# Moving one GpSimd copy, one PSUM copy and one group of transposes where batch 2 begins

## The chip, the cores and the metric

The kernel runs on one core of a Trainium2 chip. A core has five engines that run side by side, each working through its own queue in order: PE (TensorE, the matmuls and transposes), DVE (VectorE), ACT (ScalarE), POOL (GpSimd) and SP (SyncE, here only a queue that issues DMAs). They wait for each other through semaphores. PE writes to PSUM, which has eight banks; the other engines read it there. The metric is the device time of one execution in microseconds, as the median of several runs.

## The reference

For each of 8 batches and 8 heads there is x (512 rows of 64) and a state (32 rows of 64). Attention runs in both directions, and its result is the input of a two-layer network with GELU:

```python
a = softmax(x @ state.T / 8);      xread = a @ state     # 512 rows
a2 = softmax(state @ x.T / 8);     sread = a2 @ x        # 32 rows
y = concatenate([xread, sread])                          # heads side by side: 4352 rows of 512
out = gelu(y @ w_in) @ w_out                             # w_in 512x2048, w_out 2048x512
```

The output has 8 x 544 = 4352 rows of 512 in float32.

## The kernel before

The kernel never forms xread. Per batch it multiplies the state by w_in first (`p_mm`, L421: the result P has 256 rows, one for each head and state row, and 2048 columns) and then the attention weights by P. So the steps of one batch are these.

- `load_x` brings x of the batch into the tile xb by a GpSimd-issued DMA that also converts it to bf16. `rearr` (L224, two GpSimd copies) brings it into the order that the transposing DMA wants, the tile x4. `xtr_dma` (L277, issued on SP) transposes x4 into xT.
- `state_prep` (L159 and L165) transposes the state on PE, five batches at once for batches 3 to 7, and VectorE copies the result into sbd. The state comes by its own load, st_bf.
- `scores` (L330) multiplies xT by sbd and takes the exponential on ScalarE. `norm` (L350 to L353) sums, takes the reciprocal and scales on VectorE, once for each half of the heads; the scaling is L353. `atr_dma` (L373, on SP) transposes the weights a into AT.
- P is copied out of PSUM to bf16, by ScalarE for one half of the rows and VectorE for the other.
- `M(k)` is one block of the first layer (L484, two 128x512 matmuls and a GELU on ScalarE, L491). Blocks 16 to 31 belong to batch 1, block 32 is the first of batch 2.
- `U` (L510) and `X` (L581) are pieces of the second layer. Batch 0 goes plainly; from batch 1 on the second layer is done with seven products of quarter matrices (`X(b, "3")` and so on) whose operands VectorE sums first (`g_sum`, L575, and `w_sums`, L547).
- `rearr_ones` (L234, GpSimd) copies x into a third layout, xo, for `sread` (L384), which comes a whole batch later.
- `hold_for(b, m)` (L902) is a 128x1 GpSimd copy out of the output of one GELU. Its only purpose is the order: what follows it on GpSimd doesn't start before that GELU.

The order of the work is written out by hand: the kernel is a list of these calls, and each engine takes its instructions in the order of the list. The banks are part of that order. Four banks of PSUM rotate among the tiles of `ftile` (the blocks' hp, the scores, the state transposes, some P tiles); each new tile takes the bank that comes free first in the order of the list and waits until its former reader has finished. Four further banks have fixed names, o0 to o3.

Around the change, P of batch 2 is made in four tiles: p0[0] in bank o1, p0[1] in o3, p1[0] in o2, and p1[1] in a rotating bank. Three are copied by VectorE (L1093), p0[0] by ScalarE (L1095). In the kernel before, the state transposes for batches 3 to 7 take the rotating bank that p1[1] leaves, block 30 takes that of block 27, and block 31 that of block 28. `X(1, "6")` takes bank o3.

On SP's queue, `atr_dma(2)` stands ahead of `xtr_dma(3)`. On GpSimd's queue, the order before is: the load of batch 3's x, the load of the last five states, the two copies of batch 3's x (which wait for the load), `hold_for(1, 12)`, the two copies of batch 2's x into xo, `hold_for(2, 0)`, and the load of batch 4's x.

Of the kernel before, what the change touches and what calls it, by code (L numbers as in the profile page):

```python
# [17 lines left out]
def kernel(  # L18
# [8 lines left out]
    nc = tc.nc  # L27
# [51 lines left out]
    hold = persist.tile([128, 1], BF16, name="hold")  # L79
# [75 lines left out]
    def state_prep(b0, b1, pool=ps_f, tag="f"):  # L155
        n = b1 - b0
        ps = pool.tile([128, n, HC, NS], BF16, name="st_ps", tag=tag)
        for b in range(b0, b1):
            nc.tensor.transpose(  # L159
                ps[:, b - b0, :, :].rearrange("p c n -> p (c n)"),  # L160
                st_bf[:, b, :, :].rearrange("q t d -> q (t d)"),
                ident,
            )
        for t in range(2):
            nc.vector.tensor_copy(  # L165
                out=sbd[64 * t:64 * t + 64, b0:b1, :, 32 * t:32 * t + 32].rearrange(
                    "d b c n -> d (b c) n"
                ),
                in_=ps[64 * t:64 * t + 64, :, :, :].rearrange("d b c n -> d (b c) n"),
            )  # L170
# [32 lines left out]
    atts = {}  # L203

    def begin(b):
        A = Att()
        atts[b] = A
        A.x4 = x4s[b % 2]
        A.xo = xos[b % 2]
        if b > 0:  # L210
            A.xT = att.tile([128, SJ, HC, 128], BF16, name="xT", tag="xT")
# [8 lines left out]
    def rearr(b):  # L220
        A = atts[b]
        src = xbs[b].rearrange("p (t c) (j d) -> p t c j d", t=2, d=D)
        for t in range(2):
            nc.gpsimd.tensor_copy(  # L224
                out=A.x4[:, :, :, 64 * t:64 * t + 64].rearrange("p j c d -> p c j d"),
                in_=src[:, t],
            )

    def rearr_ones(b):
        A = atts[b]  # L230
        eng = nc.vector if b < 2 else nc.gpsimd
        src = xbs[b].rearrange("p (t c) (j d) -> p t c j d", t=2, d=D)
        for t in range(2):
            eng.tensor_copy(  # L234
                out=A.xo[:, :, :, 2 + 64 * t:66 + 64 * t].rearrange("p j c d -> p c j d"),
                in_=src[:, t],
            )
# [37 lines left out]
    def xtr_dma(b):  # L275
        A = atts[b]
        nc.sync.dma_start_transpose(  # L277
            out=A.xT.rearrange("p j c n -> p (j c) n"),
            in_=A.x4.rearrange("p j c n -> p (j c n)"),
        )  # L280
# [63 lines left out]
    def norm(b, half):  # L344
        A = atts[b]
        G = SJ * 2
        hs = slice(64 * half, 64 * half + 64)
        e4 = A.e[:, :, hs].rearrange("p g (c n) -> p g c n", n=NS)
        cs = att.tile([128, G, 2], FP32, name="cs", tag="cs")
        nc.vector.reduce_sum(out=cs, in_=e4, axis=AX.X)  # L350
        ics = att.tile([128, G, 2], FP32, name="ics", tag="ics")
        nc.vector.reciprocal(out=ics, in_=cs)
        nc.vector.tensor_tensor(  # L353
            out=A.a[:, :, hs].rearrange("p g (c n) -> p g c n", n=NS),
            in0=e4,
            in1=ics[:, :, :].to_broadcast((128, G, 2, NS)),
            op=ALU.mult,
        )
# [11 lines left out]
    def atr_dma(b):  # L370
        A = atts[b]
        A.AT = att.tile([128, SJ, 2, 128], BF16, name="AT", tag="AT")
        nc.sync.dma_start_transpose(  # L373
            out=A.AT.rearrange("p j t n -> p (j t) n"), in_=A.a
        )
# [39 lines left out]
    def p_mm(b, f, tiles):  # L415
        if b not in Ps:
            Ps[b] = att.tile([128, 2, d_ff], BF16, name="P", tag="P")
        ps = [tiles([128, 512], "p_ps") for t in range(2)]
        for c in range(HC):
            for t in range(2):  # L420
                nc.tensor.matmul(  # L421
                    ps[t][32 * c:32 * c + 32, :],
                    lhsT=sbd[64 * t:64 * t + 64, b, c, 32 * t:32 * t + 32],
                    rhs=w_in_bf[64 * t:64 * t + 64, c, f * 512:(f + 1) * 512],
                    start=True,
                    stop=True,
                )
        return ps
# [50 lines left out]
    def mm1(b, m):  # L479
        if m == 0:  # L480
            gs[b] = gpool.tile([128, MC, S], BF16, name="g", tag="g")
        hp = ps_f.tile([128, S], FP32, name="hp", tag="f")
        for t in range(2):
            nc.tensor.matmul(  # L484
                hp,
                lhsT=Ps[b][:, t, m * 128:(m + 1) * 128],
                rhs=atts[b].AT[:, :, t, :],
                start=(t == 0),
                stop=(t == 1),
            )  # L490
        nc.scalar.activation(out=gs[b][:, m, :], in_=hp, func=AF.Gelu)  # L491
# [57 lines left out]
    def w_sums(i):  # L549
        (b11, b12), (b21, b22) = w_q  # L550
        w_add(*(
            ("3", b12, b22, ALU.subtract),
            ("4", b21, b11, ALU.subtract),
            ("6", b11, b12, ALU.add),
            ("1", b11, b22, ALU.add),
            ("7", b21, b22, ALU.add),
        )[i])
# [343 lines left out]
    def hold_for(b, m):  # L901
        nc.gpsimd.tensor_copy(out=hold, in_=gs[b][:, m, 0:1])  # L902


    def M(*ms):
        for m in ms:
            mm1(m // MC, m % MC)
# [156 lines left out]
    U(13)  # L1064
    state_prep(2, 3, ps_o, "o3")
    w_sums(1)
    begin(3)
    rearr(3)
    M(18, 19)
    M(20, 21)  # L1070
    U(14)
# [6 lines left out]
    norm(2, 0)  # L1078
    norm(2, 1)
    atr_dma(2)  # L1080
    xtr_dma(3)
    M(24, 25)
    M(26, 27)
# [5 lines left out]

    p0 = p_mm(2, 0, home)  # L1090
    p1 = p_mm(2, 1, home)
    for f, t, ps in ((0, 1, p0), (1, 1, p1), (1, 0, p1)):
        nc.vector.tensor_copy(out=Ps[2][:, t, f * 512:(f + 1) * 512], in_=ps[t])  # L1093
    M(28, 29)
    nc.scalar.copy(out=Ps[2][:, 0, 0:512], in_=p0[0])  # L1095
    hold_for(1, 12)
    rearr_ones(2)
    state_prep(3, B)
    M(30, 31)
    nc.scalar.copy(out=xs[1, "s3"], in_=xs[1, 0])  # L1100
    X(1, "6")
    w_sums(3)
# [124 lines left out]
```

## Time and profile before

| what | value |
| --- | --- |
| median of five runs | 205.52 us (204.42 to 206.72) |
| profiled execution | 206.02 us, of which the span from the first to the last instruction is 204.3 us |
| mean granted TensorE clock | 0.999 |
| busy: PE, DVE, ACT, POOL | 196.7 (96%), 156.8 (77%), 135.5 (66%), 70.5 (35%) us |
| chain that ended last | PE 86%, DMA 5%, POOL 4%, DVE 2%, ACT 1% |
| load of batch 3's x | issued at 37.13 us, landed 10.6 us later |
| load of the last five states | issued at 38.01 us, landed 11.4 us later |

All times in the profile are in microseconds from the start of the span unless marked ns. A busy PE isn't necessarily a PE at its peak, since matmuls overlap and their ends are modelled. An instruction's idle time names what released it last. "To landing" is the time from a DMA's issue until its completion was signalled. The chain that ended last is followed backwards from the last instruction, at each step to what released it; only time on this chain can be won.

### The profile page before, as it was taken

The numbers are of one execution on the slowest core, as the hardware profiler recorded it, in microseconds if no ns is written. First come the engines' busy times: TensorE is split into PE (matmuls) and PEld (weight loads), VectorE is DVE, ScalarE is ACT, GpSimd is POOL, SyncE is SP. The second block draws the span as 40 slices with busy tenths as digits, with TensorE's granted clock in tenths as the row PEclk, the third lists the DMA queues.
The fourth block names the chain that finished last, engine by engine and source line by source line (L and its number), as shares of the span: only waits on it lengthen the run. The fifth ranks groups of instructions, "written<-read, shape, count | busy, mean of one in ns | idle before, by whom it ended". The sixth has DMA issues, their size and how long they took to land.

```text
span 204.3 us, 4903 instructions
## 1 busy us (share of the span) xinstructions
PE 196.7 (96%) x2033; PEld 133.4 (65%) x2039; DVE 156.8 (77%) x254; ACT 135.5 (66%) x240; POOL 70.5 (35%) x76
## 2 busy tenths in 40 slices
PE   7897999998999999999999999999999999999994
PEld 2442644463776667766875777667776787878893
DVE  2943677879699888977897787778778988895882
ACT  3783776689796679675966787587847666864120
POOL 8973403406619545371625702340220002200000
PEclk9999999999999999999999999999999999999999
DMA  6999997796586697836584404660107001040135
GB/s 197 187 148 203 205 200 124 120 218 162 106 119 131 188 129 85 177 138 70 58 164 126 120 0 108 77 181 3 51 3 205 3 0 55 0 157 0 51 104 157
DMA packets 40566, 23.16 MB, mean 113 GB/s; under 512 B 21856, under 2 KB 39136, under 8 KB 40544
## 3 DMA queue, kind: packets, MB, share of 16 engines
q0 software_dynamic: 13984, 8.10, 30.0%
q1 hardware_dynamic: 25872, 14.36, 28.1%
q10 hardware_dynamic: 688, 0.39, 0.6%
q8 instruction: 16, 0.26, 0.5%
q14 instruction: 6, 0.05, 0.1%
HBM read 17.30 MB, written 8.91 MB: 128 GB/s over the span
## 4 chain that ended last, share of the span: by engine, by line
PE 86%; DMA 5%; POOL 4%; DVE 2%; ACT 1%; issue 0%; POOLq 0%
PE xp L581 40%; PE hp L484 25%; DMA w_in_bf<-in_moe_w_in_dram 5%; PE p_ps L421 4%; PE op L526 4%; PE sp L788 3%; PE rp L854 3%; PE xp L693 2%; POOL w_in_bf L105 2%; PE pt L330 1%; PE sr L384 1%; PE op L510 1%; POOL sbd L95 1%; POOL w_out_bf L113 1%; DVE a L353 1%; DVE cs L350 1%
## 5 line engine op out<-in xcount | busy, mean ns | idle before, releaser
L491 ACT ACTIVATE g<-hp 128x512 bf16<-128x512 f32 x124 | 67.0, 603 | 27.1 <-PE hp L484 20.4
L484 PE MATMUL hp<-AT,P 128*128 128x512 bf16 x248 | 63.0, 379 | 0.1
L581 PEld LDWEIGHTS <-gsum 128*128 128x128 bf16 x528 | 51.1, 98 | 12.4 <-issue 1.9
L575 DVE TENSOR_TENSOR gsum<-g 128x2048 bf16<-128x2048 bf16 x35 | 45.9, 1326 | 0.9 <-ACT g L491 0.9
L581 PE MATMUL xp<-ws,gsum 128*128 128x256 bf16 x304 | 36.3, 273 | 0.0
L484 PEld LDWEIGHTS <-P 128*128 128x128 bf16 x248 | 22.9, 98 | 20.0 <-issue 2.6
L581 PE MATMUL xp<-ws,g 128*128 128x256 bf16 x224 | 26.7, 273 | 0.0
L581 PE MATMUL xp<-w_out_bf,gsum 128*128 128x256 bf16 x224 | 26.6, 273 | 0.0
L581 PEld LDWEIGHTS <-g 128*128 128x128 bf16 x224 | 21.8, 98 | 4.9 <-issue 0.2
L433 DVE CAST P<-p_ps 128x512 bf16<-128x512 f32 x29 | 18.8, 684 | 5.7 <-PE p_ps L421 5.6
L636 POOL TENSOR_TENSOR u<-s,oh 128x512 f32<-128x512 f32 x6 | 8.9, 1490 | 40.4 <-ACT oh L633 40.4
L224 POOL COPY x<-xb 128x1024 bf16<-128x1024 bf16 x12 | 13.1, 1121 | 23.2 <-DMA xb<-in_x_dram 23.2
L432 ACT CAST P<-p_ps 128x512 bf16<-128x512 f32 x29 | 15.9, 598 | 7.4 <-PE p_ps L421 7.1
L234 POOL COPY xo<-xb 128x1024 bf16<-128x1024 bf16 x12 | 15.9, 1354 | 4.2 <-PE sr L384 4.2
L600 POOL TENSOR_TENSOR v<-q,oh 128x512 f32<-128x512 f32 x6 | 8.7, 1447 | 20.8 <-ACT oh L638 20.8
L421 PE MATMUL p_ps<-w_in_bf,sbd 64*32 64x512 bf16 x248 | 10.8, 383 | 1.3 <-DMA w_in_bf<-in_moe_w_in_dram 1.3
L526 PE MATMUL op<-w_out_bf,g 128*128 128x512 bf16 x44 | 11.1, 380 | 0.5 <-issue 0.3
L353 DVE TENSOR_TENSOR a<-e,ics 128x512 bf16<-128x512 bf16 x14 | 10.4, 743 | 0.5
L350 DVE TENSOR_REDUCE cs<-e 128x16 f32<-128x512 bf16 x14 | 9.5, 677 | 0.6 <-ACT e L337 0.5
L411 DVE COPY XSR<-srT 128x128 bf16<-128x128 bf16 x8 | 5.7, 759 | 5.1 <-PE srT L408 5.1
L337 ACT ACT_TABLE_LOAD x7 | 9.0, 1283 | 0.1
L491 ACT ACT_TABLE_LOAD x7 | 9.0, 1283 | 0.1
(128 smaller groups left out, 225.9 us busy)
## 6 DMA issues: line engine op xcount, KB each, us to landing
out_dram<-oh SPq DMA_DIRECT2D x15, 256.0 KB, 2.8
xb<-in_x_dram POOLq DMA_DIRECT2D x7, 512.0 KB, 6.0
out_dram<-oh SPq DMA_DIRECT2D x6, 512.0 KB, 3.0
w_in_bf<-in_moe_w_in_dram POOLq DMA_DIRECT2D x6, 256.0 KB, 11.7
out_dram<-osb SPq DMA_DIRECT2D x5, 256.0 KB, 6.1
w_out_bf<-in_moe_w_out_dram POOLq DMA_DIRECT2D x4, 256.0 KB, 9.0
w_out_bf<-in_moe_w_out_dram POOLq DMA_DIRECT2D x2, 512.0 KB, 12.7
x0f<-in_x_dram SPq DMA_DIRECT2D x3, 256.0 KB, 3.8
```

What stands on the lines that cost most here:

```text
L224: nc.gpsimd.tensor_copy(out=A.x4[:, :, :, 64 * t:64 * t + 64].rearrange("p j c d -> p c j d"), in_=src[:, t],)
L234: eng.tensor_copy(out=A.xo[:, :, :, 2 + 64 * t:66 + 64 * t].rearrange("p j c d -> p c j d"), in_=src[:, t],)
L350: nc.vector.reduce_sum(out=cs, in_=e4, axis=AX.X)
L353: nc.vector.tensor_tensor(out=A.a[:, :, hs].rearrange("p g (c n) -> p g c n", n=NS), in0=e4, in1=ics[:, :, :].to_broadcast((128, G, 2, NS) ...
L421: nc.tensor.matmul(ps[t][32 * c:32 * c + 32, :], lhsT=sbd[64 * t:64 * t + 64, b, c, 32 * t:32 * t + 32], rhs=w_in_bf[64 * t:64 * t + 64, c ...
L432: nc.scalar.copy(out=dst[:, 0, :], in_=ps[0])
L433: nc.vector.tensor_copy(out=dst[:, 1, :], in_=ps[1])
L484: nc.tensor.matmul(hp, lhsT=Ps[b][:, t, m * 128:(m + 1) * 128], rhs=atts[b].AT[:, :, t, :], start=(t == 0), stop=(t == 1),)
L491: nc.scalar.activation(out=gs[b][:, m, :], in_=hp, func=AF.Gelu)
L526: nc.tensor.matmul(ops[b, j], lhsT=gs[b][:, m, j * 128:(j + 1) * 128], rhs=w_out_bf[:, m, :], start=(m == 0), stop=(m == MC - 1),)
L575: nc.vector.tensor_tensor(out=t, in0=g_q(b, h0, k0), in1=g_q(b, h1, k1), op=op)
L581: nc.tensor.matmul(ps[:, j - js[0], :], lhsT=lhs[:, m, 128 * j:128 * j + 128], rhs=rhs[:, m, :], start=(first and j == js[0] and m == 0), ...
```

## The change

There are three edits, all in the written-out list; no arithmetic is changed.

1. `begin(3)` and `rearr(3)` move from behind `w_sums(1)` to behind `atr_dma(2)`, and a 128x1 GpSimd copy out of batch 2's weights a is put ahead of them. That copy reads one column of the half that the second `norm` scales, so the two GpSimd copies of batch 3's x now wait for that scaling.
2. Of the three VectorE copies of P, that of p1[1] becomes the first; p0[1] is second, p1[0] third as before.
3. Blocks 30 and 31 move ahead of the state transposes. By the rotation of the banks block 30 now takes the bank that p1[1] leaves, block 31 that of block 27, and the transposes that of block 28.

```diff
     state_prep(2, 3, ps_o, "o3")
     w_sums(1)
-    begin(3)
-    rearr(3)
     M(18, 19)
     M(20, 21)
...
     norm(2, 0)
     norm(2, 1)
     atr_dma(2)
+    nc.gpsimd.tensor_copy(out=hold, in_=atts[2].a[:, 0, 64:65])
+    begin(3)
+    rearr(3)
     xtr_dma(3)
     M(24, 25)
     M(26, 27)
...
     p0 = p_mm(2, 0, home)
     p1 = p_mm(2, 1, home)
-    for f, t, ps in ((0, 1, p0), (1, 1, p1), (1, 0, p1)):
+    for f, t, ps in ((1, 1, p1), (0, 1, p0), (1, 0, p1)):
         nc.vector.tensor_copy(out=Ps[2][:, t, f * 512:(f + 1) * 512], in_=ps[t])
     M(28, 29)
     nc.scalar.copy(out=Ps[2][:, 0, 0:512], in_=p0[0])
     hold_for(1, 12)
     rearr_ones(2)
+    M(30, 31)
     state_prep(3, B)
-    M(30, 31)
     nc.scalar.copy(out=xs[1, "s3"], in_=xs[1, 0])
     X(1, "6")
     w_sums(3)
```

## The prediction

> **What bounds the kernel now.** I read the chain that ended last first, because it says which engine's time is the program's time. 86% of it is PE, and from 49.67 us to the end it is PE without a break: the idle groups name no PE wait after the one at 49.67, and TensorE's granted clock is 0.999. So a change here is worth only what it does to the time at which PE gets through the stretch from 47 to 56 us; whatever it saves or loses there shifts everything behind it by the same amount. The chain in order of time over that stretch (start, length, piece):
>
> ```profile
> 47.73 0.69 DVE a L353
> 48.42 1.21 DVE P L1093 x2
> 49.63 0.04 issue
> 49.67 0.44 PE st_ps L159 x5
> 50.11 0.86 PE hp L484 x4
> 50.98 1.75 PE xp L581 x16
> ...
> 55.78 0.47 PE pt L330 x16
> ```
>
> The chain leaves PE only here: two of the three P copies on VectorE (L1093) hold the state transposes (L159). Next I read the timelines of the engines over the same stretch (start, length, engine, line; in brackets the idle time before it and what ended it):
>
> ```profile
> 48.02 1.08 PE L484 MATMUL hp<-AT,P 128*128 128x512 bf16 x4
> 49.67 0.44 PE L159 MATMUL st_ps<-ident,st_bf 128*128 128x128 bf16 x5 [0.58 <-DVE P L1093]
> ...
> 48.94 1.28 DVE L1093 CAST P<-p_ps 128x512 bf16<-128x512 f32 x2
> 49.54 0.68 DVE L1093 CAST P<-p_ps 128x512 bf16<-128x512 f32 x1
> ...
> 47.83 2.48 POOL L224 COPY x<-xb 128x1024 bf16<-128x1024 bf16 x2 [8.87 <-DMA xb<-in_x_dram]
> 50.37 3.03 POOL L234 COPY xo<-xb 128x1024 bf16<-128x1024 bf16 x2
> ...
> 48.49 1.25 SPq L373 DMA_TRANSPOSE AT<-a  x1
> 50.34 1.85 SPq L277 DMA_TRANSPOSE xT<-x  x1
> ```
>
> To be seen: blocks 28 and 29 end, PE sits 0.58 us, then the transposes run. GpSimd's copy of batch 3's x starts at 47.83, the moment its load lands, and its end (47.83 + 2.48 = 50.31) releases the transposing DMA at 50.34. Last, the groups by tile: for xT of batch 3, and for the two-input sums on VectorE beside a GpSimd copy elsewhere in the run:
>
> ```profile
> L277 SPq DMA_TRANSPOSE xT<-x x1: 1848/1848/1848, 50.3 to 50.3; - x1
> DMA to landing us min/median/max: 4.6/4.6/4.6
> ...
> 77.94 2.03 POOL L224 COPY x<-xb 128x1024 bf16<-128x1024 bf16 x2
> 78.21 2.84 DVE L575 TENSOR_TENSOR gsum<-g 128x2048 bf16<-128x2048 bf16 x1
> ```
>
> xT lands at 50.34 + 4.6 = 54.94. The first weight load from it (scores of batch 3, L330) is at 55.50, so this transfer has only 0.56 us of slack. That number decides the case.
>
> **Copy order and the blocks put ahead of the transposes.** Nothing is added on PE or VectorE; the same instructions stand in another order. The last matmul of block 29 starts at 48.72; matmuls of this shape follow each other every 0.215 us (four in 0.86), so PE could go on at 48.94. Before, the transposes took the bank of p1[1], whose copy is second: it starts at 48.94 and PE went on at 49.67, that is 0.73 us after the start of the copy. After, block 30 takes that bank and the copy is first: it starts at 48.34, so block 30 starts at 48.34 + 0.73 = 49.07. Block 31 needs the GELU of block 27 (starts at 48.33, 0.60 long: 48.93), which is there. The two blocks take 0.86 us, to 49.93. The transposes now take block 28's bank; its GELU starts at 48.81 and ends at 49.41, so no wait, and the load of st_bf, for whose landing the weight load of the transposes waited until 49.47, is in too. Five transposes take 0.28 us (49.67 to 49.95, where block 30 followed). X(1, "6") then starts at 49.93 + 0.28 = 50.21, against 49.95 + 0.86 = 50.81: **0.60 us gained**. What the new order makes late is covered: the copy of p0[1], now second, ends at 49.62, ahead of X(1, "6") (50.21), which takes its bank; the copies into sbd end some 0.25 us later (51.4), 1.5 us ahead of their next reader on PE (52.92). If the copy order alone were made, the landing of st_bf would be next at 49.47, and only 0.2 us would be gained; the moved blocks cover it.
>
> **What is late next.** Block 32 would start at 52.56 - 0.60 = 51.96; its AT was issued at 48.49 and landed 3.1 us later, at 51.59: 0.37 us to spare. The other five AT transfers took 3.5 to 5.3 us, so this margin is thin, but those ran beside other queues' traffic. The scores of batch 3 come at 55.50 - 0.60 = 54.90, and xT already lands at 54.94 before: the slack is gone even if nothing is done to it.
>
> **The copy of batch 3's x, held.** One GpSimd instruction is added: hold, 128x1, of the rows 0.19 to 0.37 us long, which waits for the second scaling (L353, 47.73 + 0.69 = 48.42). Behind it on GpSimd stand both x copies, then hold_for(1, 12), both xo copies and the next x load; on SP's queue xtr_dma(3) waits for the x copies. An earlier hold ran 0.14 us behind its GELU, and its successor started 0.13 us behind it (50.24, 50.37). So the copies start at 48.42 + 0.1 + 0.13 = 48.65 (48.8 with the longest hold), 0.8 us later. But the first copy took 1.495 us against 1.037 for the shortest of this line, because it ran into the scaling until 48.42; held, it doesn't. Both together then take 2.03 us, as at 77.94: the end is 50.68 to 50.85, I take 50.73. xtr_dma(3) goes at 50.76 instead of 50.34, **0.42 us later**. Its duration is not shown for that start: the six transfers of L277 landed 4.2, 4.4, 4.6, 4.9, 5.4 and 6.1 us after issue. Bounds are 4.2 and 6.1; I take 4.6, the row of the same batch, as nothing else moves on the DMA engines at that time (their share is 0 from 54.25 on, and AT's packets are through at 51.05). xT lands at 55.36, and PE waits 55.36 - 54.90 = **0.46 us lost**. The xo copies slip to 50.9 and beside the weight sum of VectorE at 51.4; at worst (both copies first, as at 78.21) that sum ends near 54.2, the P copy behind it at 54.8 and the operand sum at 56.0, still ahead of X(1, "5") at 56.35. The next x load goes near 54.8 rather than 54.49; xT of batch 4 landed over 9 us before its use. So these cost nothing.
>
> One rule speaks to the hold. The rows come first: at 78.21 a two-input sum of 1.21 us (the shortest of its line) took 2.84, having come 0.27 us behind two GpSimd copies that together last 2.03; it was held 1.63 us. At 47.83 the copy came 0.10 us behind the scaling, and the copy was held. The Trainium skill, "SBUF — State Buffer", section "Who interferes with whom", says that a VectorE instruction with two SBUF inputs and a GpSimd instruction that reads SBUF exclude each other, and that whichever starts first keeps the port for its whole instruction. By that rule the sum at 78.21 would have been free after the first copy, an estimated 0.8 us, and an x copy ahead of the scaling would cost the kernel before one copy at most. The row at 78.21 shows both copies. In the profiled execution the scaling came first, so this price is not in the sum; where the load lands 0.1 us or more sooner, the row puts it at 0 to 1.63 us on the path through AT and the P copies.
>
> **Sum.** -0.60 + 0.46 = -0.14 us. The profiled execution took 206.02 us (span 204.3 and 1.7 around it), so it would become 205.88. It is 0.50 above the median of the five runs, which lie from 204.42 to 206.72; against the median the forecast is 205.52 - 0.14 = **205.4 us**, its own range 205.2 (xT in 4.4 us) to 205.5 (the longest hold, or xT in 4.7).
>
> **Rivals.**
> (a) The whole gain or more. If xT lands 4.2 us after issue (54.96), PE waits 0.06 and 0.54 us are gained: 205.0. If the load of batch 3's x commonly lands sooner than in the profiled execution, the kernel before also pays for the copy ahead of the scaling: between 0 and 1.63 us by the row at 78.21, and with the middle, 0.8, that gives 204.2. For it: the margin seen was 0.10 us. Against: only one execution shows the landing.
> (b) Slower: the held copy makes xT the bound. PE reaches the scores later than before as soon as 50.76 + d is over 55.50, that is d over 4.74 us. Three of the six transfers are over that. With d = 5.4, the scores come at 56.16: 0.66 us lost, 206.2; if the kernel before had the same d, the difference is 0.42, 205.9. Against: the slow ones had output traffic near them.
> (c) The change does not do what it says: the copy order still leaves PE waiting, since GELUs 24 to 28 sit end to end on ScalarE (46.88 to 49.41). Then it gains 0 to 0.1 and loses nothing beyond the slack of 0.56: 205.5.
>
> **Chances.** Forecast 0.40, (a) 0.28, (b) 0.27, (c) 0.05. About 1% of the time (2.06 us) is what a measurement of this kernel can tell from no change; no case reaches that alone. Only landings that shift several waits at once would, so faster 0.05, same 0.90, slower 0.05. The range runs from (a) with most of the port's middle price (205.0 - 0.6; 204.42 is also the fastest run before) to (b) with 0.66 and 0.2 for the scatter of a median over few runs that lie 2.3 us apart: 204.4 to 206.4.
>
> **What the profile after would show.** Right: no PE idle time ahead of L159; block 30 near 49.07; X(1, "6") near 50.2; L224's two copies 2.0 to 2.1 us long from about 48.65; a new PE wait of about 0.5 us at L330 near 54.9, released by xT's transfer. Wrong: PE waiting at block 32 for AT (a late transpose); no wait at L330 (case a); a wait over 1.06 us there (case b); L224 still at 1.5 us, or GpSimd's hold much later than 48.6.

## The result and the profile after

The changed kernel takes 206.12 us (median of 43 runs) against 205.74 us for the kernel before (80 runs). The ratio is 1.0018 with a 95% interval of 1.0003 to 1.0032: **slower by 0.4 us, between 0.06 and 0.66**. The forecast was a gain of 0.14 us. So the time lies inside the range, on the wrong side, and the case that came true is rival (b). That (b)'s 206.2 us lies near the measured time is partly luck: it stood for a loss of 0.66 us from 205.52, and the kernel before came out at 205.74.

The profiled execution took 207.21 us, with a span of 205.4 us. Its chain that ended last, in order of time (start, length, piece), no longer leaves PE for the P copies. It leaves it for the copy of batch 3's x and the transfer of xT:

```profile
47.48 0.70 DVE a L353
...
48.30 0.19 POOL hold L1079
48.49 0.74 POOL x L224
49.23 0.18 issue
49.41 1.04 POOL x L224
50.45 0.03 POOL hold L902
50.47 5.77 DMA xT<-x
56.24 0.05 issue
56.29 0.64 PE pt L330 x16
```

The timelines of PE, VectorE, GpSimd and SP over the same stretch:

```profile
47.76 2.08 PE L484 MATMUL hp<-AT,P 128*128 128x512 bf16 x8
49.68 0.44 PE L159 MATMUL st_ps<-ident,st_bf 128*128 128x128 bf16 x5
49.96 1.91 PE L581 MATMUL xp<-ws,gsum 128*128 128x256 bf16 x16
...
56.29 0.64 PE L330 MATMUL pt<-sbd,xT 128*128 128x64 bf16 x16 [1.36 <-DMA xT<-x]
...
48.42 2.03 POOL L224 COPY x<-xb 128x1024 bf16<-128x1024 bf16 x2
...
50.47 1.93 SPq L277 DMA_TRANSPOSE xT<-x  x1
```

PE runs blocks 28 to 31, the transposes and X(1, "6") without a gap: the stall of 0.58 us is gone. In its place PE waits 1.36 us at the scores of batch 3. The group by tile says why:

```profile
L277 SPq DMA_TRANSPOSE xT<-x x1: 1927/1927/1927, 50.5 to 50.5; - x1
DMA to landing us min/median/max: 5.8/5.8/5.8
```

The transfer took 5.8 us, not 4.6. The profiled executions in this document differ by up to 2.4 us in how soon batch 2 gets there, ahead of the stretch that the change is about. Below I therefore use one measure that leaves the start out: the **stretch** from batch 2's first sum on VectorE (L350) to the scores of batch 3 on PE (L330). Before it is 55.62 - 45.11 = 10.51 us, after 56.29 - 44.86 = 11.43 us.

### The profile page after: what moved, and what is told of

It reads as the page before. It is cut to its first block, busy times and chain, and to the rows that moved or that the text cites. A ratio compares the mean times of both kernels' runs of the same rounds, so it can differ in the third digit from the quotient of the medians.

```text
span 205.4 us, 4905 instructions
## 1 busy us (share of the span) xinstructions
PE 197.1 (96%) x2033; PEld 133.4 (65%) x2039; DVE 157.5 (77%) x254; ACT 135.4 (66%) x240; POOL 69.3 (34%) x77
## 4 chain that ended last, share of the span: by engine, by line
PE 82%; DMA 9%; DVE 3%; ACT 2%; POOL 1%; issue 1%; POOLq 0%
PE xp L581 38%; PE hp L484 23%; DMA xb<-in_x_dram 5%; PE p_ps L421 4%; PE op L526 3%; PE sp L788 3%; PE rp L854 3%; DMA xT<-x 3%; PE xp L693 2%; DMA st_f<-in_state_dram 2%; PE pt L330 1%; PE sr L384 1%; PE op L510 1%; POOL x L224 1%; DVE a L353 1%; DVE cs L350 1%
## 5 line engine op out<-in xcount | busy, mean ns | idle before, releaser
L636 POOL TENSOR_TENSOR u<-s,oh 128x512 f32<-128x512 f32 x6 | 7.8, 1305 | 40.8 <-ACT oh L633 40.8
L224 POOL COPY x<-xb 128x1024 bf16<-128x1024 bf16 x12 | 12.6, 1082 | 14.0 <-DMA xb<-in_x_dram 14.0
L350 DVE TENSOR_REDUCE cs<-e 128x16 f32<-128x512 bf16 x14 | 9.5, 677 | 0.4 <-ACT e L337 0.3
```

The lines of the kernel that those rows point to most:

```text
L224: nc.gpsimd.tensor_copy(out=A.x4[:, :, :, 64 * t:64 * t + 64].rearrange("p j c d -> p c j d"), in_=src[:, t],)
```

## The experiments

Each kernel ran beside the kernel before on the same chip, and its ratio is against that. Theory A says that the hold is the loss, by starting xT later. Theory B says that the load of batch 4's x, which PE's lead brings forward, runs into xT's transfer.

### Which part, and is it the next load?

**Edits 2 and 3 alone.** The hold is left out and the x copies stay where they were:

```diff
     w_sums(1)
+    begin(3)
+    rearr(3)
...
-    nc.gpsimd.tensor_copy(out=hold, in_=atts[2].a[:, 0, 64:65])
-    begin(3)
-    rearr(3)
     xtr_dma(3)
```

> Edits 2 and 3 alone (copy order, blocks 30 and 31 ahead of the transposes); the copies of batch 3's x start when their load lands, as before. Theory A (the hold is the loss: xT starts 0.4 us later and takes its usual 4.6 us): xT issued near 50.3, landing near 54.9, PE reaches its scores at 54.9 with at most 0.2 us of waiting, 0.4 to 0.6 us faster than before. Theory B (the load of batch 4's x, which PE's lead brings forward to about 53.8 us, runs into the tail of xT's transfer and delays its end by about 1.2 us): xT lands 5.5 to 6 us after issue here too, PE waits about 1.2 us at the scores of batch 3, and the time is 0.3 to 0.7 us slower than before, hold or no hold.

Measured: ratio 0.998 (0.9946 to 1.0015). xT was issued at 49.81 and landed 4.6 us later; PE waited for nothing at the scores of batch 3, and the stretch was 10.07 us. The next load went at 53.88, as early as in the changed kernel. The transfer is as theory A has it, and B's collision didn't show. The ratio stands for a gain of 0.4 us, which is inside the interval; the medians, 205.78 against 205.73 us, show none.

**Edit 1 alone.** The hold and the moved copies, on the kernel before:

```diff
     w_sums(1)
-    begin(3)
-    rearr(3)
...
     atr_dma(2)
+    nc.gpsimd.tensor_copy(out=hold, in_=atts[2].a[:, 0, 64:65])
+    begin(3)
+    rearr(3)
     xtr_dma(3)
```

> Edit 1 alone (the hold and the moved copies). Theory A: xT is issued 0.4 us later and lands at 55.4, just inside its slack of 0.56 us: no difference, within 0.2 us. Theory B: the load of batch 4's x stays behind PE's block 32 at 54.5 us or later, behind the end of the transfer's packets at 54.2 to 54.6, so again no difference; if the later transfer still meets the load, up to 0.8 us slower.

Measured: ratio 1.0025 (0.9999 to 1.0051). xT took 6.0 us, PE waited 1.01 us at the scores and the stretch was 11.68 us. This is more than theory A's 0.4 us of lateness, which the slack should have taken up. The load went at 53.02, so B was still possible.

**All edits, with the next load put off:**

```diff
                 hold_for(b, 0)
+                for _ in range(8 if b == 2 else 0):
+                    hold_for(b, 0)
                 load_x(4 if b == 2 else b + 3)
```

> All three edits, and eight more 128x1 GpSimd copies ahead of the load of batch 4's x, which put its issue about 1 us later (near 54.9 instead of 53.8). Theory A: no change against the changed kernel, xT still lands 5 to 6 us after issue and PE waits about 1.4 us. Theory B: xT lands 4.4 to 4.8 us after issue, the wait at the scores falls to 0.2 to 0.5 us, and the time is 0.1 to 0.2 us below the kernel before, about 0.5 to 1 us below the changed kernel.

The eight copies took 0.63 us each on average, where the expectation had counted about 0.13, so the load went at 57.83, after the scores had begun. **xT still took 5.8 us and PE still waited 1.36 us.** Theory B falls: the load wasn't there and the delay was. The time itself (209.53 us, ratio 1.016, 1.0123 to 1.0196) says nothing on B. With the load so late PE waited another 1.6 us near 69.5, behind sums of VectorE, and in this profile TensorE's granted clock was 0.50 from 71.35 to 74.75 us, where it is 1.00 in the profiles of the two kernels. What ties the two together was not tried.

**The kernel before, with the next load put ahead:**

```diff
-                hold_for(b, 0)
+                hold_for(*((1, 15) if b == 2 else (b, 0)))
```

> The kernel before with one thing changed: the hold ahead of the load of batch 4's x reads the GELU of block 31 instead of block 32, so that the load goes about 0.6 us earlier (near 53.8 instead of 54.5). Theory A: nothing happens, since GpSimd is off the chain and xT is issued as before: within 0.1 us. Theory B: xT lands 5.5 to 6 us after issue, PE waits 0.4 to 0.8 us at the scores of batch 3, and the time is slower than before by as much.

Measured: ratio 1.0018 (0.9994 to 1.0042). The load went at 51.59, in the middle of xT's transfer, which took 4.7 us, and PE didn't wait at the scores. As a test of B this is weak, since the load's first packets started at 53.19, behind the last of xT's at 53.03. The changed kernel says more: there too the load's first packets (55.42) come only after xT's last (55.14). But the stretch was 11.08 us, and the reason is another one, which the prediction had left out of its sum. Batch 3's x had landed at 44.4 us in this execution, and GpSimd's copies met the first scaling. The scalings in VectorE's timeline of this kernel, and then its row in the list of waits (total, times, longest):

```profile
44.75 1.26 DVE L353 TENSOR_TENSOR a<-e,ics 128x512 bf16<-128x512 bf16 x1
46.94 0.69 DVE L353 TENSOR_TENSOR a<-e,ics 128x512 bf16<-128x512 bf16 x1
...
PE st_ps L159 <- DVE P L1093: 1.1, 1, 1.1
```

The first scaling took 1.26 us in place of 0.69, everything behind it on VectorE came as much later, and PE waited 1.1 us ahead of the transposes instead of 0.58.

### What delays xT: PE's own instructions

With A too small and B fallen, I looked at the DMA queues in short windows (queue, kind: packets, MB, share of 16 engines in the window). The kernel before, from 54.15 to 54.40 us:

```profile
q8 instruction: 1, 0.02, 23.3%
q1 hardware_dynamic: 6, 0.00, 2.2%
```

The changed kernel, from 54.15 to 54.40 us, and then from 54.40 to 55.20:

```profile
q8 instruction: 1, 0.02, 22.6%
q1 hardware_dynamic: 28, 0.00, 10.6%
...
q1 hardware_dynamic: 4, 0.00, 1.2%
```

q1 holds xT's packets. q8 is a fetch of instructions: a single packet of 16 KB, which keeps one of the 16 engines busy for 0.226 x 16 x 0.25 = 0.90 us. In the kernel before it starts as xT's packets end, and nothing of q1 follows. In the changed kernel four packets of q1 follow 0.9 us later, and xT can't be complete before them. The part of the page on the queues shows 16 such packets, 0.26 MB, in every execution. From the fourth to the last of them PE goes from instruction 953 to 4009 of its queue in the kernel before, 255 a packet. In every profile the earliest of them start when PE stands 157 to 161 instructions into a block of 256; for the fourth block that is near instruction 929 (an estimate of where the fetch is asked for, since the request itself isn't traced). **Theory C**: PE's next instructions are fetched when PE reaches that place in its queue, and where this falls early enough in xT's transfer, the last packets of xT stand behind the fetch on that engine.

PE reaches that place 2.0 us after xT's packets begin in the kernel before, and 1.0 us after in the changed one, because PE got faster and xT later. If C holds, adding PE instructions at the very start moves the fetch and nothing else. The warm-up matmuls of the first microseconds, whose results nobody reads, can be cut up for this:

```diff
     def keep_warm(n):
         ps = otile([128, 512], "warm_ps")
         while n > 0:
-            w = 128 * min(n, 4)
+            w = 128
...
-            n -= 4
+            n -= 1
```

> All three edits, and the warm-up matmuls at the start cut into 128 columns each, which adds 45 matmuls with their weight loads, 90 PE instructions, and no time. PE's instructions come from memory by 16 KB transfers (256 instructions each, 0.9 us on one DMA engine); the one that PE asks for near its instruction 930, 1.0 us into xT's transfer, is moved 90 instructions earlier, to about 47 us, ahead of both transposes. Theory C (the last packets of xT stand behind this fetch): xT lands 4.4 to 4.8 us after issue, PE waits 0.2 to 0.5 us at the scores of batch 3 instead of 1.4, and the time is 0.5 to 1.0 us below the changed kernel, 0 to 0.2 us below the kernel before. Theory A (the transfer's length has nothing to do with PE's instruction count): 5.6 to 6.0 us and a wait of 1.2 to 1.4 us, as in the changed kernel.

Measured: 204.12 us, **ratio 0.9916 (0.9887 to 0.9946)**. The fetch went at 47.01 us, xT took 4.3 us, and after the first wait of the program PE waited for nothing at all. Rows by tile and by wait of this kernel:

```profile
L277 SPq DMA_TRANSPOSE xT<-x x1: 1842/1842/1842, 49.3 to 49.3; - x1
DMA to landing us min/median/max: 4.3/4.3/4.3
...
PE warm_ps L149 <- DVE warm L92: 1.2, 1, 1.2
```

The stretch is 9.92 us: 10.51 less 0.59, which is the gain that the prediction had for the new order (0.60). The expected wait of 0.2 to 0.5 us didn't come, as the transfer was 0.3 us shorter than the row I had taken. The time fell by more than this: 1.85 us between the medians. Against a kernel before whose load lands early (11.06 us, below) the stretch gains 1.14; the rest is open.

**The reverse: the kernel before, with 12 PE instructions more.** `keep_warm(28)` gets its first eight pieces cut to 128 columns; nothing of the change is in it.

> The kernel before, with 6 warm-up matmuls more (two of 512 columns cut into eight of 128): 12 PE instructions, and no time. The fetch that PE asked for 2.0 us into xT's transfer is now asked for about 0.7 us into it. Theory C: the fetch comes ahead of xT's last packets, xT lands 5.4 to 6.0 us after issue instead of 4.6, PE waits 0.3 to 0.8 us at the scores of batch 3, and the time is slower by 0.3 to 0.7 us, with not one instruction of the change in it. Theory A: nothing changes.

Measured: the fetch at 53.38, then two more packets of q1 at about 54.3, xT 5.9 us instead of 4.6, and a wait of PE at the scores (L331 here) that the kernel before doesn't have. The queues from 53.3 to 53.5 us and from 53.6 to 54.4, the row of xT, and PE's timeline of this kernel:

```profile
q8 instruction: 1, 0.02, 29.3%
...
q1 hardware_dynamic: 2, 0.00, 0.4%
...
DMA to landing us min/median/max: 5.9/5.9/5.9
...
55.45 0.64 PE L331 MATMUL pt<-sbd,xT 128*128 128x64 bf16 x16 [0.51 <-DMA xT<-x]
```

The stretch was 11.18 us, 0.67 longer. **Twelve instructions at the start make xT late in a kernel that is otherwise the same**, in one profile of each. In the times it is too little to be seen: ratio 1.0008 (0.9978 to 1.0037), where 0.3 to 0.7 us were expected.

**Edits 2 and 3 with the 90 instructions:**

> Edits 2 and 3 without the hold, and the 90 PE instructions of warm-up. Theory C: the fetch is out of the way and the x copies start when the load lands, so xT lands 4.4 to 4.8 us after issue near 50 us, PE waits at most 0.1 us: 0.4 to 0.7 us faster than before, the best of all. Theory A: as edits 2 and 3 alone, 0 to 0.6 us faster.

Measured: ratio 0.9967 (0.9936 to 0.9998), 205.11 us. xT took 4.3 us and PE didn't wait for it. But this was not the best: without the hold the x copies met the first scaling (1.38 us), PE waited 0.66 us for the P copy ahead of block 30, and the stretch was 10.60 us, 0.68 longer than with the hold.

**The kernel before with the 90 instructions, the control:**

> The kernel before with the 90 PE instructions of warm-up alone, as a control. Both theories: no wait at the scores of batch 3 either way, so no difference, within 0.3 us; where the other runs of the kernel before do meet the fetch now and then, up to 0.3 us faster by theory C.

Measured: ratio 0.9987 (0.9958 to 1.0016), no difference. So the longer warm-up alone is not the gain. Here too the load had landed early (44.7 us), the first scaling took 1.25 us, and the stretch was 11.06.

### What the hold is worth, and the comparison side by side

**Edit 1 alone, with the 90 instructions** (the diffs of the two kernels above together):

> Edit 1 alone (the hold and the moved copies) on the kernel before, with the 90 PE instructions of warm-up, so that no fetch meets xT. Theory P (the hold is worth something because GpSimd's copies of batch 3's x otherwise run into the scaling on VectorE, which took 1.25 to 1.38 us instead of 0.69 where the load landed early): the scalings take 0.69 us both, PE waits 0.57 us ahead of the state transposes, not 1.1, and the time is 0.3 to 0.8 us below the kernel before. Theory Q (the hold is a pure cost of 0.4 us on xT, which the slack takes up): no difference, within 0.2 us.

Measured: 204.75 us, **ratio 0.9957 (0.9927 to 0.9987)**, as theory P has it. Both scalings took their usual time, and PE waited the known 0.57 us. VectorE's timeline of this kernel:

```profile
45.66 0.69 DVE L353 TENSOR_TENSOR a<-e,ics 128x512 bf16<-128x512 bf16 x1
47.26 0.69 DVE L353 TENSOR_TENSOR a<-e,ics 128x512 bf16<-128x512 bf16 x1
```

The stretch of this profile is 10.50 us, as in the first profile of the kernel before, in which the load happened to land late. What the hold takes away is the early case, 11.06 to 11.08 us.

**All edits with the 90 instructions, again:**

> All three edits and the 90 PE instructions once more, now beside the changed kernel itself. Theory C: 1.0 to 2.0 us faster than the changed kernel, 1.0 to 1.8 us faster than the kernel before; xT lands 4.2 to 4.6 us after issue, no wait at the scores of batch 3.

Measured: 204.06 us, ratio 0.994 (0.9918 to 0.9963); xT 4.3 us, no wait, stretch 9.92.

**The changed kernel, again** (no edit):

> The changed kernel itself, for a comparison on the same chip. Theory C: xT lands 5.6 to 6.0 us after issue, PE waits 1.2 to 1.4 us at the scores of batch 3; 0.1 to 0.6 us slower than the kernel before.

Measured: 205.71 us, ratio 1.0014 (0.9986 to 1.0041); xT 5.6 us, 1.21 us of waiting, stretch 11.28. So the two differ by 1.65 us in the median. The stretch accounts for 1.36 of them; batch 2's own xT made PE wait some 0.5 us more in this profile of the changed kernel.

**All edits with 42 instructions more** (only the 28 first warm-up pieces are cut):

> All three edits with 42 PE instructions of warm-up more instead of 90 (the first 28 warm-up pieces cut to 128 columns), which moves the same fetch from xT's transfer into AT's, about 0.5 us after that begins. Theory C: AT lands 3.8 to 4.6 us after issue instead of 3.1, PE waits 0.2 to 0.9 us for it at block 32, and xT is free again (4.2 to 4.6 us); the time lies between the changed kernel and the one with 90 instructions. Theory A' (any longer warm-up helps, by the state of the start): as fast as with 90 instructions, AT at 3.1 us.

Measured: 205.82 us, ratio 1.0003 (0.9971 to 1.0035), with single runs from 204.13 to 209.06 us. The fetch did fall into AT's transfer, at 51.9 us. But it started as AT's packets ended, and AT took its 3.1 us: this part of theory C's expectation failed. xT was free (4.4 us) and the stretch was 10.10 us. Why the median is not lower is open. In this profile PE waited 1.9 us for casts of the first batch's x, and the granted clock was 0.50 from 8.50 to 11.90 us, where the kernel before has 1.00. Its mean over the profile is 0.992; the five of the twelve runs with that mean took 206.45 to 209.06 us, the other seven 204.13 to 206.09. None of the theories speaks of this part of the start.

### All stretches together

| kernel | first scaling | xT, us from issue | stretch, us |
| --- | --- | --- | --- |
| before | 0.69 | 4.6 | 10.51 |
| before, next load earlier | 1.26 | 4.7 | 11.08 |
| before, 90 instructions | 1.25 | 4.4 | 11.06 |
| before, 12 instructions | 0.69 | 5.9 | 11.18 |
| edit 1 alone | 0.69 | 6.0 | 11.68 |
| edit 1, 90 instructions | 0.69 | 4.2 | 10.50 |
| edits 2 and 3 alone | 0.86 | 4.6 | 10.07 |
| edits 2 and 3, 90 instructions | 1.38 | 4.3 | 10.60 |
| all, three profiles | 0.69 | 5.8, 5.8, 5.6 | 11.43, 11.43, 11.28 |
| all, 90 instructions, two profiles | 0.69 | 4.3, 4.3 | 9.92, 9.92 |
| all, 42 instructions | 0.69 | 4.4 | 10.10 |

Three terms explain the column but for the last row's 0.18 us: -0.59 for the new order, +0.15 to +0.68 where the copies meet the scaling (which the hold removes), and +0.67 to +1.5 where the fetch comes ahead of xT's last packets.

## Why the prediction was wrong

**Right: the copy order and the blocks.** The working had 0.60 us. From the first sum to X(1, "6") it is 50.81 - 45.11 = 5.70 before and 49.96 - 44.86 = 5.10 after.

**Right: the held copy starts xT later.** 0.42 us were predicted. From the first sum to xT's issue it is 50.34 - 45.11 = 5.23 before and 50.47 - 44.86 = 5.61 after, 0.38 more. The two x copies took 2.03 us, as read from the row at 77.94.

**Wrong: "I take 4.6, the row of the same batch, as nothing else moves on the DMA engines at that time".** This is the step that failed. It was 5.8, and PE waited 1.36 us for it instead of 0.46: the scores came 11.43 us after the first sum, where the same kernel with nothing in the way has 9.92. Something did move: one packet of PE's instructions, which in the kernel before starts just as xT's last packets end. The prediction took the same batch's transfer for a quantity that belongs to the batch, while it was a near miss. The reading behind the step was wrong too: a DMA share of 0 from 54.25 us on doesn't mean idle engines, since the view counts a packet where it starts, and the fetch started at 54.24 and lasted 0.93 us (23.3% of 16 engines in 0.25 us). With 4.3 us, the value without the fetch, the stretch gained the whole 0.59.

**Rival (b) had xT as the bound and the threshold** (slower as soon as the transfer takes over 4.74 us), but no reason for a long transfer, and a wrong argument against it: "the slow ones had output traffic near them". The trace of the kernel before had the better one. Its fetches at 39.2, 92.0, 114.4 and 127.3 us lie inside transfers that took 6.1 us (xT issued at 35.18), 5.2 (AT, 90.15), 5.3 (AT, 111.44) and 5.4 (xT, 125.01); those that no fetch met took 3.1 to 3.6 for AT and 4.2 or 4.4 for xT. One xT of 4.9 (issued at 103.76) had only a fetch ahead of it. The control with the 90 instructions, in which nothing else is changed, bears this out. Its fetches miss three of those transfers, and these are shorter: 4.6 (xT issued at 34.58), 3.7 (AT, 89.71) and 4.4 (xT, 124.58). The AT of 111 us still meets one and takes 5.2, and the AT of 132 us, which met none before, now has a fetch at 135.1 and is longer. In all fourteen profiles this AT takes 4.6 to 5.2 us with the 90 instructions and 3.3 to 3.7 without. Its rows in the kernel before, and then in the control:

```profile
L373 SPq DMA_TRANSPOSE AT<-a x1: 1288/1288/1288, 132.8 to 132.8; - x1
DMA to landing us min/median/max: 3.5/3.5/3.5
...
L373 SPq DMA_TRANSPOSE AT<-a x1: 1291/1291/1291, 132.4 to 132.4; - x1
DMA to landing us min/median/max: 5.1/5.1/5.1
```

The sign given for (b), a wait of over 1.06 us, doesn't fit (b)'s own threshold, which stands for a wait of 0.60 us (55.50 - 54.90).

**Missing from the sum: the port.** The price of a copy ahead of the scaling was given as 0 to 1.63 us and entered as 0, because the profiled execution had the scaling first by 0.10 us; an early landing was the condition of rival (a). In the four later profiles without the hold and with an early landing it was 0.17 to 0.69 us on the first scaling; where it was over 0.5, the stretch was 0.55 to 0.68 longer. In all four the scaling ended 0.53 to 0.55 us after the first copy did, so it was held by one copy, not by both as the sum at 78.21 was, and the 1.63 us at the upper end of the price was not seen. A median over runs of the kernel before probably contains some of this term. That would account for a measured loss of 0.4 us where the two first profiles differ by 0.92 us in the stretch, but how often the load lands early was not measured.

The Trainium skill, "Runtime: NRT & Kernel Launch", section "Instruction fetch mechanics", says that each engine's instructions are refilled in blocks of 16 KiB, 256 instructions, by a DMA queue that the sequencer drives, and that crossing a block boundary is mostly hidden. The runs agree on the block (packets of 16 KB, 255 instructions apart). On the cost they show something else: the lists of PE's waits put at most 0.3 us down to no known cause ("issue"), but a transfer that PE does wait for came 1.3 to 1.8 us later.

**Left open.** What decides whether the fetch comes ahead of a transfer's last packets. By the estimate above, asked for 0.8 to 1.6 us after xT's first packets it did, at 1.9 to 2.5 us it didn't, and half a microsecond into AT's it didn't either. Whether the order depends on how many of the transfer's packets are already lined up was not tried. Nor is the whole delay explained: the packets behind the fetch came 0.9 us late in the changed kernel, but from the last packet to the landing it was another 1.1 us, against 0.7 in the kernel before and 0.5 with the 90 instructions.

## What to carry to other kernels

Where a wait is taken off the path, measure the slack of the next transfer, and then look at what else is on the DMA engines within a microsecond of its end, instruction fetches included: here PE's came at nearly the same places of its queue in every profile, so a change in the instruction count or in the order can bring them in or move them out. A change that measures as nothing or as a small loss may be sound and lose its gain to such a meeting; here the same three edits are 0.8% and 0.6% faster than the kernel before, in two comparisons, once 90 instructions that alone make no measured difference are put at the start. A transfer's time in one profile is a sample, and its price belongs in the sum with the spread of its kind.

## What the runs showed of the hardware that was not expected

- A fetch of 256 PE instructions holds one of the 16 DMA engines for 0.9 us, and can put off the completion of another transfer by 1.3 to 1.8 us (xT 5.6 to 6.0 us in place of 4.2 to 4.6, compared between kernels that differ in the instructions at the start alone).
- Two GpSimd copies and a two-input sum on VectorE delayed each other according to who started first: scalings of 0.69 us took 1.25 to 1.38 us when a copy had begun 0.20 to 0.34 us earlier, and 0.86 us when it had begun 0.72 us earlier.
- All edits with the 90 instructions gave 203.99 to 204.68 and 203.85 to 204.74 us in eight runs each, while the kernel before, beside them, ranged over more than 3 us in 31. That the spread shrinks because both delays are gone is not shown: edit 1 with the 90 instructions, which has neither, gave 204.44 to 205.47 us and one run of 207.82 (granted clock 0.983).
